# Transposing key and query weights by DMA from DRAM, issuing early loads from two queues, and a new order of work in a conditioned transformer block

## The chip, the cores and the metric

The kernel runs on one core of one Trainium2 chip. The metric is device time in microseconds (us) of one launch. Three runs of the kernel before took 207.98, 208.01 and 208.36 us, so the median is 208.01.

A core has five engines that run their own instruction queues side by side: PE (matrix products; its weight loads are listed apart as PEld), DVE (vector work), ACT (scalar functions and copies), POOL (further elementwise work) and SP, which here only issues DMA transfers. ACT can issue transfers too. Each engine works through its queue strictly in order and waits at an instruction until the semaphores that it names have arrived.

## What is computed

A block with 2048 tokens of width 512: a first half with linear attention over 32 heads of 16 columns, a second half with a gated layer of width 1376. A condition vector c gives six modulation vectors.

```python
mod = (silu(c) @ w_mod).reshape(1, 6, 1, -1)          # sa, ca, ga, sb, cb, gb
h = layernorm(x) * (1 + ca) + sa
q, k, v = heads of h @ wqkv
pq, pk = q @ w_phi, k @ w_phi                         # 16x16 per head
phi = concat(softmax(p), softmax(-p))                 # for q and for k
kv, z = phi_k.T @ v, phi_k.sum(tokens)
x = x + ga * ((phi_q @ kv) / (phi_q @ z) @ wo)
h = layernorm(x) * (1 + cb) + sb
x = x + gb * ((sigmoid(h @ w_gate) * (h @ w_up)) @ w_down)
```

## The kernel before

**Tiling.** Tokens are cut into 16 tiles of 128. x, all weights and the normalised, transposed h1T stay in on-chip memory. Keys and queries use weights that are folded first: wqk_f is wk (or wq) times the block-diagonal matrix bd of w_phi, so that one product gives pk directly.

**The order is written out by hand.** Every piece of work is a task in a graph: `G.add(name, {engine: cost}, fn, r=..., w=..., bufs=...)` names the engines that may run it, what it reads and writes and which buffers it holds. The long string `ORDER` (lines 37 to 78) lists every task once; `arrange` walks it, gives each task the engine after its `@` (or the first of its table) and hands out buffer slots first come, first served, and `emit` then writes the instructions. So each engine's queue is the ORDER string filtered by engine. The costs in the tables play no part when the kernel runs.

**DMA transfers.** `load` (line 659) makes a load task, always on SP. Each transfer signals one of eight semaphores, used in rotation; a transfer whose semaphore is still in use by an older one waits at its issuing engine until that older one has landed.

**The start.** ACT issues the loads of c and w_phi (lines 229 and 231) and loads its function table (line 232). PE runs dummy products (`warm`). The tasks that matter here:

- `ld_x0b`, `ld_x0a`, ... (lines 663, 664): x in pieces of two tiles. `st1_t` (lines 799, 800, DVE): mean and variance of tile t. `rs1_g` (806, 807 on ACT, 809, 810 on POOL) and `nmr1_g` (815, DVE): reciprocal deviation and shift of a group g of one or two tiles. `xn1_t` (824 ACT, 826 DVE, 828 POOL): the normalised tile. `tphgj` (841, PE) transposes column block j of group g, and `hm1_gj` (848 ACT, 850 DVE) applies the modulation on the way to h1T. Groups 6 and 7 are transposed by DMA instead (`xT1_t`, 833).
- `ld_wk0`, `ld_wk1` (670): the key weights. `tpwk` (759, PE) transposes them in blocks, `wTck` (763, ACT) copies the result to wT_sb. `fold1i` (776, PE) multiplies by bd, `foldc1i` (782 ACT, 784 DVE) writes wqk_f. Each fold reads all four wT blocks.
- `ld_wq0` (676), `wqTk` (769): the query weights, loaded and then transposed by DMA from on-chip memory to on-chip memory.
- `c1`, `c2`, `c3`: silu(c). `ld_wm00`, `ld_wm01` (667): the columns of w_mod for sa and ca, by halves of the rows. `modc1.0`, `modc1.1` (735, PE) and `modc1c` (741, 742, ACT): sa and 1 + ca.

**The attention stage.** Per tile: `Kt` (867, PE, four 512-column products, one for each row block j), `et` (883, ACT, two exponentials), `nt` (886, DVE, sums), `rt` (896, 897 on ACT or 899 on DVE, reciprocal), `phit` (889, POOL or DVE), `Vt` (871, PE), `vat` (907, ACT or DVE), `kvt` (280, PE, accumulates over all tiles). Queries: `Q` (945, PE), `qe` (950, ACT). When all 16 `kv` are in, `kvm` (301, DVE), `kvp` (316, PE) and the copies to kvbd follow.

**The rest.** For each tile numerators, division, projection with wo, second normalisation; then in six chunks of tokens g and u (574, PE), tanh (584, ACT), the product (595, DVE), y (612, PE), `fin` (619, DVE) and the store `st` (621, SP). `modc2.0`, `modc2.1` (735) compute the second set of modulation vectors. Tile 15's y is cut in 384 and 128 columns, and the 128 columns come last.

Of the kernel before, what the change touches and what calls it, by code (L numbers as in the profile page):

```python
# [38 lines left out]
wTc0 nmr1_2 st1_4 ld_wk1 tpw3 warm1_8 tpw2 wTc2 xn1_3@P bd ld_x2a st1_5 xn1_2@P nmr1_1 st1_0 warm1_9 warm1_10 warm1_11 warm1_12 wTc3 rs1_0 ld_wm00 ld_wm01  # L39
st1_9 c3 st1_8 xn1_0 warm1_13 warm1_14 fold11 ld_x2b fold13 fold12 fold10 modc1.0 ld_wv0 foldc11 foldc13 foldc10 modc1.1 tph20 rs1_3@P xn1_1@P ld_x1b rs1_5@P  # L40
foldc12@D modc1c tph21 tph11 tph22 warm1_15 nmr1_3 xn1_5@P xn1_4@P hm1_21 hm1_20@A hm1_22 tph03 tph23 tph10 tph01 tph00 hm1_10 hm1_23@A K2 hm1_00@A ld_wq0
tph02 hm1_01@A hm1_03@A ld_wd2 ld_wmga ld_x3a wqT2 nmr1_5 xn1_8@P xn1_9@P st1_10 st1_11 tph13 K3 tph12 rs1_6@P hm1_02@A hm1_11@A hm1_12 st1_7 tph33 tph30 K0
hm1_13@A wqT0 wqT3 wqT1 e2.0 st1_6 nmr1_6 hm1_33 n2.0 rs1_4@P e0.0 e3.0 hm1_30@A nmr1_4 tph32 V2 K1 tph53 V3 tph52 tph31 hm1_53 hm1_32 xn1_11@P hm1_31 e1.0
# [4 lines left out]
qe10 n7.0 r8.0 xn1_12@P xT1_12 va6@D r7.0 phi6.0 xn1_15@P tph83 kv5.0 ld_wg0 ld_wo tph80 kv6.0 tph81 hm1_83 e11.2 hm1_81 hm1_71@P phi7.0 hm1_72@A e10.0
hm1_70@A hm1_73@A V8 n9.0 hm1_80 V10 va8@D n10.0 e11.4 va9 r9.0@A phi8.0 e11.0 e11.6 n11.2 n11.0 r10.0 n11.6 V13 kv7.0 tph82 r11.6 r11.0 n11.4 hm1_82@A K12
K13 kv8.0 va10 e13.4 r11.2 ld_wu0 e13.0 phi9.0 n13.4 r11.4 r13.4 n13.0 e12.0 phi10.0 K15 Q11 ld_wd kv9.0 V14 phi11.0@D n12.0 e15.4 r13.0@A K14 kv10.0 phi11.2  # L50
phi11.4 phi11.6 e15.0 va13 Q03 Q01 e14.4 r12.0@A va14 e14.0 phi13.4@D phi13.0 phi12.0 n14.4 n14.0 r14.4@A r14.0 n15.0 n15.4 r15.4 phi14.4@D V12 kv11.4 Q13
modc2.0 va12 qe01 phi14.0 phi15.4@D qe13 r15.0@A kv11.0 kv11.6 kv11.2 gra kv12.0 V15 Q02 kv13.4 va15 qe03 phi15.0@D kv14.4 kv13.0 kv15.4 kv14.0 kvm1 kv15.0
Q32 kvm0 qe02 perm kvp2 kvp1 kvp0 kvz2 kvz1 kvz0 kvn0 modc2.1 sm0 sm2 qe32 modc2c kvn2@A kvn1@A wo2 smS2 smS0@D den0 den2 Q12 Q31 qe31 wo3 num00 qe11 num30
num01 Q30 num31 u00 u01 Q23 num20 u30 u31 qe12 u20 tpo0 num21 u21 oT0 wo1 wo0 wo_all sm1 smS1 o3 sm4 smS4 num10 out0 num11 den1 x1_0 qe30 qe23 Q33 Q21 Q22
num61 qe33 u11 st2_0 u10 o2 tpo1 rs2_0 gwb nmr2_0 den4 num70 u70 qe21 oT1 num71 xn2_0 u71 grb wd0 qe22 Q20 out1 wd10 xnT0 num60 x1_1 mod00 mod01 wd4 wd5 wd1
# [24 lines left out]
bndc u5.10 u5.3 hm5.9 hm5.8 y11.9 y11.10 bndd u5.1 tg5.3 tg5.1 hm5.3 fin11 hm5.1 g5.10 ldf y12.0 y14.0 y14.1 y14.2 y14.3 y14.4 y14.5 y14.6 y14.7 y14.8 y14.9  # L80
# [77 lines left out]
def kernel(  # L158
# [92 lines left out]
    def engine(e):  # L251
        return {"PE": pe, "ACT": act, "DVE": dve, "POOL": pool, "SP": sp}[e]
# [406 lines left out]
    def load(name, key, fn, nbytes):  # L659
        G.add("ld_" + name, {"SP": 0.45}, fn, w=key, nbytes=nbytes)  # L660
# [473 lines left out]
```

## Time and profile before

| | |
|---|---|
| median of 3 runs | 208.01 us |
| the profiled execution | 208.63 us |
| its span, first to last instruction | 206.9 us |
| busy of PE, DVE, ACT, POOL | 199.4, 168.8, 110.1, 96.3 us |
| granted PE clock | 0.999 |
| moved by DMA | 19.27 MB |

The span begins with the first instruction and ends with the last; 1.73 us of the device time lie around it. The sums of the prediction are made in the span of the profiled execution. In the views an entry gives the start (us from the span's start), the busy time (us), the engine, the source line and what is written and read; "SPq" and "ACTq" are the issues of transfers on those queues, and "idle before" names what the engine waited for last.

### The profile page before, as it was taken

How to read it: one execution, taken by the hardware profiler on the slowest of the kernel's cores; microseconds unless marked ns; L12 is line 12 of the kernel's file. 1: busy time of each engine (PE TensorE's matmuls, PEld its weight loads, DVE VectorE, ACT ScalarE, POOL GpSimd, SP SyncE). 2: the span in 40 equal slices, each digit the busy share in tenths (PEclk: the TensorE clock that was granted, in tenths of full speed). 3: DMA queues.
4: the chain of work that ended last, by engine and by line, in shares of the span. 5: the costliest groups of instructions: out<-in, count | busy, mean ns of one | idle time of the engine just before them, and what ended most of it. 6: DMA issues, size and time to landing. Idle time of an engine off the chain costs nothing.

```text
span 206.9 us, 4373 instructions
## 1 busy us (share of the span) xinstructions
PE 199.4 (96%) x1539; PEld 112.8 (54%) x1563; DVE 168.8 (82%) x462; ACT 110.1 (53%) x267; POOL 96.3 (47%) x128
## 2 busy tenths in 40 slices
PE   7889999999999999999999999999999999999993
PEld 2465554554676689768764544454444444444442
DVE  3999999998989998999999999898797865235632
ACT  2689999999979986433343543231523351144100
POOL 5787999999976987774256000014400220000000
PEclk9999999999999999999999999999999999999999
DMA  6999877697101211205321121141223022000111
GB/s 161 341 351 237 106 194 261 183 382 242 55 0 54 51 32 25 54 0 103 72 49 34 39 42 25 26 91 39 52 51 76 5 51 76 0 0 29 33 52 54
DMA packets 32557, 19.27 MB, mean 93 GB/s; under 512 B 21169, under 2 KB 30738, under 8 KB 32530
## 3 DMA queue, kind: packets, MB, share of 16 engines
q1 hardware_dynamic: 32000, 18.92, 34.3%
q8 instruction: 14, 0.23, 0.5%
q14 instruction: 13, 0.11, 0.2%
q10 hardware_dynamic: 530, 0.02, 0.1%
HBM read 12.11 MB, written 2.10 MB: 69 GB/s over the span
## 4 chain that ended last, share of the span: by engine, by line
PE 71%; ACT 18%; DMA 4%; DVE 3%; SPq 2%; issue 1%; DVEq 0%; ACTq 0%
PE y_ps L612 18%; PE u_ps L574 17%; PE g_ps L574 17%; ACT e L883 8%; PE a_ps L483 7%; PE q_ps L945 4%; ACT h1T L848 4%; DMA wmod_sb<-in_w_mod_dram 4%; ACT vaug L907 3%; PE num L366 2%; PE num L450 2%; DVE phi L889 1%; PE g_ps L576 1%; SPq L664 1%; DVE ks L886 1%
## 5 line engine op out<-in xcount | busy, mean ns | idle before, releaser
L584 ACT ACTIVATE tg<-g_ps 128x512 bf16<-128x512 f32 (+5 forms) x66 | 28.9, 454 | 58.0 <-PE g_ps L574 38.1
L612 PE MATMUL y_ps<-wd_sb,wmod_sb 128*128 128x512 bf16 (+4 forms) x184 | 43.8, 366 | 0.2
L595 DVE SCALAR_TENSOR_TENSOR wmod_sb<-tg,u_ps 128x512 bf16<-128x512 bf16 (+4 forms) x63 | 30.0, 494 | 15.0 <-ACT tg L584 7.3
L574 PEld LDWEIGHTS <-wu_sb 128*128 128x128 bf16 (+1 forms) x252 | 21.7, 99 | 15.7 <-issue 0.2
L574 PEld LDWEIGHTS <-wg_sb 128*128 128x128 bf16 (+1 forms) x252 | 21.5, 99 | 14.7 <-issue 0.2
L889 POOL TENSOR_TENSOR phi<-e,ks 128x1024 bf16<-128x1024 bf16 (+2 forms) x17 | 27.7, 1637 | 1.1 <-DVE ks L899 0.3
L612 PEld LDWEIGHTS <-wmod_sb 128*128 128x128 bf16 (+1 forms) x187 | 17.4, 98 | 16.9 <-issue 0.2
L574 PE MATMUL u_ps<-wT_sb,wu_sb 128*128 128x512 bf16 (+2 forms) x122 | 23.7, 321 | 0.1
L574 PE MATMUL g_ps<-wT_sb,wg_sb 128*128 128x512 bf16 (+2 forms) x122 | 23.7, 321 | 0.1
L503 POOL TENSOR_SCALAR ve<-mv 128x2 f32<-128x2 f32 (+1 forms) x8 | 1.8, 223 | 42.3 <-DVE mv L493 42.3
L574 PE MATMUL u_ps<-wqk_sb,wu_sb 128*128 128x128 bf16 (+4 forms) x127 | 19.9, 287 | 0.1
L886 DVE TENSOR_REDUCE ks<-e 128x64 f32<-128x1024 bf16 (+2 forms) x22 | 19.7, 903 | 0.3 <-ACT e L883 0.2
L574 PE MATMUL g_ps<-wqk_sb,wg_sb 128*128 128x128 bf16 (+4 forms) x127 | 19.6, 287 | 0.1
L883 ACT ACTIVATE e<-k_ps 128x512 bf16<-128x512 f32 (+2 forms) x44 | 18.4, 500 | 0.0
L950 ACT ACTIVATE eT<-q_ps 128x512 bf16<-128x512 f32 x32 | 16.8, 611 | 1.8 <-PE q_ps L945 1.7
L474 POOL TENSOR_TENSOR o<-u 128x512 bf16<-128x512 f32 x10 | 12.6, 1269 | 9.5 <-DVE u L456 4.2
L619 DVE TENSOR_TENSOR ot<-y_ps,x 128x512 bf16<-128x512 f32 (+2 forms) x17 | 11.2, 656 | 6.9 <-PE y_ps L612 6.6
L483 PE MATMUL a_ps<-wo_sb,oT 128*128 128x512 bf16 x57 | 15.7, 379 | 0.4
L945 PE MATMUL q_ps<-h1T,wqk_f 128*128 128x512 bf16 x62 | 15.7, 379 | 0.1
L867 PE MATMUL k_ps<-wqk_f,h1T 128*128 128x512 bf16 x63 | 15.5, 379 | 0.1
L871 PE MATMUL v_ps<-wv_sb,h1T 128*128 128x512 bf16 x59 | 15.2, 379 | 0.2
L799 DVE BATCH_NORM_STATS2 st<-x_sb 128x6 f32<-128x512 bf16 x16 | 10.8, 673 | 2.6 <-DMA x_sb<-in_A_x_dram 2.6
(156 smaller groups left out, 334.7 us busy)
## 6 DMA issues: line engine op xcount, KB each, us to landing
out_dram<-ot SPq DMA_DIRECT2D x15, 128.0 KB, 1.8
x_sb<-in_A_x_dram SPq DMA_DIRECT2D x6, 256.0 KB, 5.0
wmod_sb<-in_w_mod_dram SPq DMA_DIRECT2D x3, 512.0 KB, 6.5
wmod_sb<-in_w_mod_dram SPq DMA_DIRECT2D x1, 1536.0 KB, 10.3
wg_sb<-in_B_w_gate_dram SPq DMA_DIRECT2D x1, 1376.0 KB, 7.1
wd_sb<-in_B_w_down_dram SPq DMA_DIRECT2D x1, 1280.0 KB, 13.9
wu_sb<-in_B_w_up_dram SPq DMA_DIRECT2D x1, 768.0 KB, 11.0
wu_sb<-in_B_w_up_dram SPq DMA_DIRECT2D x1, 608.0 KB
```

Source lines behind the costliest of these rows:

```text
L483: pe.matmul(ap_[:], lhsT=oT[:, j, :], rhs=wo_sb[:, j, :], start=(j == 0), stop=(j == KT - 1))
L574: pe.matmul(ps[:fsz, 0:n], lhsT=w[:, j, ft * P:ft * P + fsz], rhs=h[:, j, 0:n], start=(j == 0), stop=(j == KT - 1))
L584: G.add(f"tg{k}.{ft}", {"ACT": 0.13 + n * 0.00083}, lambda e, tg=tg, g_ps=g_ps, fsz=fsz, n=n: act.activation(tg[:fsz, 0:n], g_ps[:fsz, 0:n ...
L595: dve.scalar_tensor_tensor(hm_all[:fsz, hm[k].slot, ft, 0:n], tg[:fsz, 0:n], 1.0, u_ps[:fsz, 0:n], op0=ALU.add, op1=ALU.mult)
L612: mm = pe.matmul(y[:, 0:c1 - c0], lhsT=hm_all[:fsz, hm[k].slot, ft, tl * P:(tl + 1) * P], rhs=wd_sb[:fsz, ft, c0:c1], start=(ft == 0), sto ...
L867: pe.matmul(kp[:], lhsT=h1T[:, j, t * P:(t + 1) * P], rhs=wqk_f[:, j, D:2 * D], start=(j == 0), stop=(j == KT - 1))
L871: pe.matmul(vp[:], lhsT=h1T[:, j, t * P:(t + 1) * P], rhs=wv_sb[:, j, :], start=(j == 0), stop=(j == KT - 1))
L883: act.activation(ee[:, ha:hb, s, :], kp[:, ha * DH:hb * DH].rearrange("p (h j) -> p h j", j=DH), ACT.Exp, scale=1.0 - 2.0 * s)
L886: dve.tensor_reduce(ks[:, ha:hb].rearrange("p h s -> p (h s)"), ee[:, ha:hb].rearrange("p h s j -> p (h s) j"), axis=AX.X, op=ALU.add)
L889: engine(e).tensor_tensor(ph[:, ha * 32:hb * 32].rearrange("p (h j) -> p h j", j=DH), ee[:, ha:hb].rearrange("p h s j -> p (h s) j"), ks[: ...
L945: pe.matmul(qp[:], lhsT=wqk_f[:, j, blk * P:(blk + 1) * P], rhs=h1T[:, j, cq * 512:(cq + 1) * 512], start=(j == 0), stop=(j == KT - 1))
L950: act.activation(eT[cq][:, s * 4 + blk, :], qp[:], ACT.Exp, scale=1.0 - 2.0 * s)
```

## The change

- **Weights straight from DRAM** (`DIRECT = [1, 1]`). `ld_wk0`, `ld_wk1`, `tpw0` to `tpw3`, `wTc0` to `wTc3` and `ld_wq0` go. Instead `wkT0` to `wkT3` and `wqT0` to `wqT3` are DMA transposes on SP that read 128 rows of A_wqkv in DRAM and write one row block of wT_sb for all head columns. A fold now waits for its own row block only.
- **Two issuing queues.** The loads of x and of the first modulation weights may stand on ACT. In the new order ACT issues `ld_x0a`, `ld_x1a`, `ld_wm00a`, `ld_wm00b`, behind c and w_phi; the function table load becomes a task `actl` and stands behind them.
- **Modulation by column halves.** `ld_wm0ih` loads 256 columns of sa (a) or ca (b); `modc1.h` and `modc1ch` finish two of the four column blocks each, and `hm1_gj` waits for its half only. An array `mone` lets DVE do `modc1ch`; the order leaves it on ACT.
- **Products in halves.** `K0` to `K7` and `V0` to `V3` become `Kta`, `Ktb` (row blocks 0 and 1, then 2 and 3), each waiting for its own blocks.
- **Smaller loads**: wv, w_gate, x3 and wo in two pieces each, w_down's ten full blocks in two.
- **A new ORDER** for every engine. Among its moves: `phi9.0` and `phi12.0` (full tiles) and `phi11.4`, `phi14.0`, `phi15.0`, `phi15.4` stand on DVE (before: `phi11.0`, `phi13.4`, `phi14.4`, `phi15.0`, `phi15.4`); `xn1_13` and `xn1_15` stand on DVE; both halves of `modc2` stand ahead of `kv15`; the y products of tile 14 now come last.

```diff
+KSP = 8
+DIRECT = [1, 1]
+VSP = 4
-SPLIT = {"wk": 2, "wv": 1, "wq": 1, "wg": 1, "wu": 2, "x1": 2, "x2": 2, "x3": 1}
+SPLIT = {"wk": 2, "wv": 2, "wq": 2, "wg": 2, "wu": 2, "x1": 2, "x2": 2, "x3": 2, "wo": 2}
...
-wdz warm0 pmem ld_x0b st1_2 st1_3 ld_x0a c1 warm1_0 warm1_1 warm1_2 warm1_3 warm1_4 warm1_5 warm1_6 warm1_7 st1_1 c2 rs1_2 rs1_1 ld_x1a ld_wk0 tpw1 tpw0 wTc1
+wdz warm0 c1 warm1_0 warm1_1 warm1_2 warm1_3 warm1_4 warm1_5 warm1_6 warm1_7 warm1_8 warm1_9 warm1_10 warm1_11 ld_x0a@A pmem bd ld_x0b st1_2 st1_3 ld_x1a@A
+ld_wm00a@A ld_wm00b@A wkT1 wkT2 st1_1 st1_0 wkT0 actl ld_wm01a rs1_2 rs1_1 c2 nmr1_1 nmr1_2 xn1_2@P fold12 fold11 warm1_12 c3 rs1_0 xn1_3 xn1_1@P tph21
+modc1.0 ld_x2a foldc12 foldc11 modc1c0 st1_4 st1_5 tph10 tph20 tph13 tph11 warm1_13 ld_wm01b xn1_0 hm1_20 rs1_3@P tph00 tph02 warm1_14 tph03 fold10 hm1_00
+hm1_11@A hm1_21@A hm1_10@A wkT3 ld_x1b warm1_15 tph22 tph23 tph01 ld_x2b modc1.1 nmr1_3 xn1_5@P xn1_4@P foldc10 K3a hm1_01@A modc1c1 hm1_03@A hm1_22@A st1_8
...
-    act.preload_act_table_set("natural_log_exp_and_others")
...
+        G.add("ld_" + name, {"SP": 0.45, "ACT": 0.45} if act else {"SP": 0.45}, fn, w=key, nbytes=nbytes)
...
+        for s in range(2):
+            c = s * D + 256 * i
+            load(f"wm0{i}{'ab'[s]}", [("wmod0", i, s)], lambda e, c=c: engine(e).dma_start(wmod_sb[:, :, c:c + 256], wmod_v[:, :, c:c + 256]), 256 * K1, True)
...
+    G.add("actl", {"ACT": 1.19}, lambda e: act.preload_act_table_set("natural_log_exp_and_others"), w=["actl"])
...
+            if side == 1 and DIRECT[1]:
+                G.add(f"wkT{k}", {"SP": 1.2}, lambda e, k=k: sp.dma_start_transpose(wT_sb[:, 1, :, k * P:(k + 1) * P], A_wqkv[k * P:(k + 1) * P, D:2 * D]),
+                      w=[("wT", 1, k)], nbytes=-1)
...
+                if DIRECT[0]:
+                    G.add(f"wqT{k}", {"SP": 1.2}, lambda e, k=k: sp.dma_start_transpose(wT_sb[:, 0, :, k * P:(k + 1) * P], A_wqkv[k * P:(k + 1) * P, 0:D]),
+                          w=[("wT", 0, k)], nbytes=-1)
...
-            G.add(f"fold{side}{kt_in}", {"PE": 0.24}, f3, r=[("wT", side, k) for k in range(KT)] + ["bd"], w=[("fold", side, kt_in)], bufs=[ps])
+            G.add(f"fold{side}{kt_in}", {"PE": 0.24}, f3, r=[("wT", side, kt_in), "bd"], w=[("fold", side, kt_in)], bufs=[ps])
...
+        if t < KSP:
+            for h in range(2):
+                js = (2 * h, 2 * h + 1)
+                G.add(f"K{t}{'ab'[h]}", {"PE": 0.435}, lambda e, js=js, f=f_k: f(e, js), r=[h1k[j] for j in js] + [("wqk", j, 1) for j in js], w=[("k", t)], bufs=[kp])
```

The instructions on PE that do the computation stay the same but for the 16 transposes of `tpw`.

More of the change, by code (lines that the diff above doesn't have):

```diff
@@ L40 @@
[L40 to L43, printed above, removed]
@@ L48 @@
[L48 to L51, printed above, removed]
@@ L52 @@
[L52 to L55, printed above, removed]
@@ L738, in modc_task, with modc1_task, f, f2 @@
         G.add(nm + "c", {"ACT": dur}, lambda e: f2(ps), r=[nm + "ps"], w=wk, bufs=[ps])
-    def f_mc1(ps):
-        act.copy(modc[:, 0:4], ps[:, 0:4])
-        act.add(modc[:, 4:8], ps[:, 4:8], 1.0)
+    def modc1_task(h):
+        ps = bank("modc_ps", [P, 2, 2])
+        dst = modc[:, 0:8].rearrange("p (s j) -> p s j", s=2)[:, :, 2 * h:2 * h + 2]
+        def f(e):
+            for j in range(KT):
+                for s in range(2):
+                    for i in range(2):
+                        c = s * D + (2 * h + i) * P
+                        pe.matmul(ps[:, s, i:i + 1], lhsT=wmod_sb[:, j, c:c + P], rhs=sc_bf[:, j:j + 1],
+                                  start=(j == 0 and s == 0 and i == 0), stop=(j == KT - 1), skip_group_check=True)
+        def f2(e):
+            if e == "ACT":
+                act.copy(dst[:, 0], ps[:, 0])
+                act.add(dst[:, 1], ps[:, 1], 1.0)
+            else:
+                dve.tensor_tensor(dst, ps[:], mone[:], op=ALU.add)
+        G.add(f"modc1.{h}", {"PE": 0.4}, f, r=[("wmod0", h, 0), ("wmod0", h, 1), "scbf"], w=[("mc1ps", h)], bufs=[ps])
+        G.add(f"modc1c{h}", {"ACT": 0.35, "DVE": 0.15}, f2, r=[("mc1ps", h)], w=[("mod1", h)], bufs=[ps])
     def f_mc2(ps):
@@ L810, in f_rs @@
                 pool.tensor_tensor(rs1[:, sl], ve1[:, sl], mhalf[:, sl], op=ALU.pow)
-        G.add(f"rs1_{g}", {"ACT": 0.43, "POOL": 1.1}, f_rs, r=[("mv1", t) for t in ts], w=[("rs1", g)])
+        G.add(f"rs1_{g}", {"ACT": 0.43, "POOL": 1.1}, f_rs, r=[("mv1", t) for t in ts] + ["actl"], w=[("rs1", g)])
         if g:
```

147 lines of the change are left out of this document (82 added, 65 removed).

## Prediction

> **What bounds the kernel now.** I read the page first: busy times, then the chain of work that ended last.
>
> ```profile
> PE 199.4 (96%) x1539; PEld 112.8 (54%) x1563; DVE 168.8 (82%) x462; ACT 110.1 (53%) x267; POOL 96.3 (47%) x128
> PE 71%; ACT 18%; DMA 4%; DVE 3%; SPq 2%; issue 1%; DVEq 0%; ACTq 0%
> ```
>
> PE carries 71% of the chain, but it is an average over stages. The chain in order of time shows them:
>
> ```profile
> 4.45 7.29 DMA wmod_sb<-in_w_mod_dram
> 11.79 0.57 PE modc_ps L735 x16
> 12.65 3.19 ACT h1T L848 x8
> ...
> 53.10 1.32 DVE phi L889
> 54.54 1.34 DVE phi L889 x2
> 56.23 0.86 PE q_ps L945 x4
> 57.10 0.50 PE kvp L316 x16
> 57.60 0.66 PE modc_ps L735 x24
> ...
> 194.16 9.56 PE y_ps L612 x55
> ```
>
> The start waits for modulation weights (to 11.79). The attention stage then runs on ACT and ends on three DVE phi; from 56.23 to the last y at 203.7 there is nothing but PE. The windows say how tight each stage is (columns: length, then busy time of PE, PEld, DVE, ACT, POOL):
>
> ```profile
> 13.84:55.80 41.96, 41.28 (x364) 22.98 (x368) 40.22 (x84) 41.40 (x108) 39.51 (x38) 1.00 0.80 217
> 3.62:55.80 52.18, 50.12 (x462) 28.41 (x468) 49.57 (x114) 48.10 (x126) 46.23 (x49) 1.00 0.85 240
> 56.00:203.70 147.70, 146.80 (x1072) 83.53 (x1089) 118.50 (x347) 60.50 (x141) 47.22 (x60) 1.00 0.18 42
> ```
>
> From 13.84 to 55.80 all four engines are busy over 94% of the time. That is the key to this change: in this stage an earlier start of PE returns nothing unless DVE, ACT and POOL also end earlier. After 56 PE idles visibly for 147.70 - 146.80 = 0.90 us, so a better order there can return about that.
>
> **The front.** Timeline of the first stage (start, busy), then what the tile and line views say of landings:
>
> ```profile
> 0.80 1.48 SPq L664 DMA_DIRECT2D x_sb<-in_A_x_dram  x3
> 1.36 0.44 ACTq L231 DMA_DIRECT2D wp_sb<-in_A_w_phi_dram  x1
> 1.84 1.28 ACT L232 ACT_TABLE_LOAD   x1 [1.84 <-issue]
> 3.62 0.69 DVE L799 BATCH_NORM_STATS2 st<-x_sb 128x6 f32<-128x512 bf16 x1 [2.43 <-DMA x_sb<-in_A_x_dram]
> 4.45 0.66 DVE L799 BATCH_NORM_STATS2 st<-x_sb 128x6 f32<-128x512 bf16 x1
> 5.42 0.30 ACT L806 ACTIVATE ve<-mv,eps 128x2 f32<-128x2 f32 x1 [1.05 <-DVE mv L800]
> 6.15 0.29 ACT L806 ACTIVATE ve<-mv,eps 128x1 f32<-128x1 f32 x1 [0.20 <-DVE mv L800]
> 10.28 1.56 ACT L782 CAST wqk_f<-fold_ps 128x512 bf16<-128x512 f32 x3
> 13.49 0.81 PE L867 MATMUL k_ps<-wqk_f,h1T 128*128 128x512 bf16 x3
> ```
>
> ```profile
> L769 SPq DMA_TRANSPOSE wT_sb<-wqk_sb x4: 1266/1274/1335, 16.4 to 20.3; - x4
> DMA to landing us min/median/max: 2.9/4.2/5.3
> ```
>
> ```profile
> L833 SPq DMA_TRANSPOSE h1T<-xn x4: 1189/1230/1268, 21.7 to 35.7; - x4
> DMA to landing us min/median/max: 2.4/2.4/3.2
> ```
>
> Now the new queue of ACT: c, w_phi (issued until 1.80), x0a, x1a, wm00a, wm00b, the table load, and only then rs1_2. In the built program wm00a waits until x0b has landed and wm00b until wkT1 has, because the eight transfer semaphores are used in turn. x0b is still SP's first issue and lands at 3.62, where the first statistics start. wkT1 is SP's second: issued from 0.80 + 1.48/3 = 1.29 on, for 1.27 us. Its landing is the unknown of this stage, since no trace shows a transpose that reads DRAM: the rows of transposes that read on-chip memory give 2.4 to 5.3 us. I take 3.2, the slowest of the h1T rows, since wkT1 has a load of x in front of it as well, and keep 2.4 and 5.3 as ends. So wkT1 lands at 4.5, wm00b is issued until 5.0, the table is loaded at 6.3 (in before it was hidden, 1.84 to 3.12), and rs1_2 starts at 6.3 instead of 5.42: **0.9 later**.
>
> What follows on ACT ahead of K3a: three pairs of rs1 (5.42 to 6.15 less the 0.20 waited is 0.53 each, 1.6), c2 (0.2), xn1_3 (0.8, row below), foldc12, foldc11, foldc10 (1.56/3 each, 1.6), a modc pair (about 0.3) and three hm1 of one or two tiles (3.19/8 each, 1.2): 5.7 in all, so K3a starts near 12.0, against 13.49. PE's front is 1.5 earlier. What goes (16 tpw transposes, 4 wTc copies, two key loads) lay beside the wait for w_mod. SP's four wkT cost 4 x 1.27 = 5.1 us of issue ahead of the later x loads, wv and the rest; x2a is issued near 5.6 instead of 3.38, and its readers st1_8 and st1_9 come after 11. That is cover enough as long as x2a lands within 5.4 us; beyond that DVE would wait by the difference. Halves of K and V move no work, the 128 products stay; they let K start on two row blocks.
>
> **The stage on DVE.** DVE starts at 3.62 as before, and I count what the new order gives it. Groups by form (count | busy us, mean ns):
>
> ```profile
> L850 DVE TENSOR_SCALAR h1T<-tp_h,modc 128x256 bf16<-128x256 bf16 x11 | 4.1, 394 | 0.6 <-ACT modc L742 0.3 <-PE tp_h L841 0.2
> L899 DVE RECIPROCAL ks<-ks 128x64 f32<-128x64 f32 x7 | 3.8, 542 | 0.1
> L889 DVE TENSOR_TENSOR phi<-e,ks 128x512 bf16<-128x512 bf16 x4 | 3.3, 855 | 0.7 <-POOL phi L889 0.5
> L824 ACT ACTIVATE xn<-x_sb,nmr,rs 128x512 bf16<-128x512 bf16 x2 | 1.6, 812 | 0.0
> L850 DVE TENSOR_SCALAR h1T<-h1T,modc 128x256 bf16<-128x256 bf16 x3 | 1.0, 383 | 0.0
> L826 DVE TENSOR_SCALAR xn<-x_sb,mv,rs 128x512 bf16<-128x512 bf16 x1 | 0.4, 381 | 0.0
> ```
>
> ```profile
> L889 DVE TENSOR_TENSOR phi<-e,ks x5: 424/693/1311, 47.0 to 55.2; 128x512 bf16<-128x512 bf16 x4, 128x256 bf16<-128x256 bf16 x1
> ```
>
> It loses one half phi (0.86), one reciprocal (0.54), one h1T out of PSUM (0.39) and two h1T in place (0.77): -2.56. It gains two xn (0.76) and two full-tile phi (phi9, phi12). A full phi on DVE isn't in the trace; it is twice a half one: 2 x 0.69 to 2 x 1.31, at the mean 1.71. So DVE's work grows by 0.76 + 3.42 - 2.56 = **+1.6** (bounds +1.0 and +3.4). The half phi took 0.69 where DVE had waited for POOL's to end, and 1.31 at 53.10, with POOL's own phi running.
> The Trainium skill, "SBUF — State Buffer", section "Who interferes with whom", has the reason: a DVE instruction with two on-chip inputs and a POOL instruction that reads on-chip memory exclude each other, and the later one blocks. The two lengths agree with it. By that page a full phi could wait out a whole POOL phi on top and the sum would end above my upper bound.
>
> DVE's idle time was 52.18 - 49.57 = 2.61, of which 41.96 - 40.22 = 1.74 after 13.84. At the front the four first statistics end at 3.62 + 4 x 0.8 = 6.8, and nmr1_1 now waits for rs1_1 at 6.3 + 2 x 0.53 = 7.4: +0.6. Of the 1.74 I let 1.1 go, since DVE is now behind everyone and its waits for POOL's phi (0.5 in its row) shrink as POOL gives two phi away. That is a choice; the bounds are 0 and all 1.74. So the last phi ends 1.6 + 0.6 - 1.1 = **1.1 later**, near 56.9. ACT doesn't relieve this: its modulation starts about 2.5 earlier, but it takes one fold copy, two v copies, three more reciprocal pairs and another rs1 pair, some 3 to 4 us, and ends later too. POOL's relief (two phi) helps nobody, as it doesn't end last.
>
> So PE's 1.5 earlier start turns into waiting at the last kv products.
>
> **After the stage.** One half of modc2 (0.66, the chain's row at 57.60) has moved ahead of kv15, into that waiting: **-0.66**. Tail, from the view of the output tile and of the transfers:
>
> ```profile
> L619 DVE TENSOR_TENSOR ot<-y_ps,x x6: 291/688/692, 192.7 to 203.7; 128x512 bf16<-128x512 f32 x4, 128x384 bf16<-128x384 f32 x1, 128x128 bf16<-128x128 f32 x1
> ```
>
> ```profile
> out_dram<-ot SPq DMA_DIRECT2D x15, 128.0 KB, 1.8
> ...
> out_dram<-ot SPq DMA_DIRECT2D x1, 32.0 KB, 1.8
> ```
>
> Before, the last y is 128 columns wide and its fin takes 0.29; now it is a whole tile, 0.69: **+0.40**. The stores land in 1.8 either way. The other loads (w_gate, wo, w_down in pieces, wq without its copy) are hidden: after 56 the DMA engines are busy 18%.
>
> **Sum:** +1.1 - 0.66 + 0.40 = +0.8 on the profiled 208.63 (1.73 outside its span of 206.9). The median of the runs shown is 0.62 lower: 208.01 + 0.8 = **208.8**.
>
> **Rivals.**
> 1. *Faster: DVE keeps up.* If its full phi cost only 1.38 and all later idle time goes, the stage ends 1.0 + 0.6 - 1.74 = 0.1 earlier; if the new order also returns half of PE's visible 0.90, the sum is -0.1 - 0.66 + 0.40 - 0.45 = -0.8: 207.2. For it: POOL has slack now, so the exclusion can resolve in DVE's favour. It decides where the last phi ends less than 0.26 later than before. PE's whole 1.5 can't come through: DVE would have to do 49.57 + 1.6 in 50.7 us.
> 2. *Much slower: transposes from DRAM land late.* At the 5.3 us of the wT_sb row wkT1 lands 2.1 later; ACT stands in front of wm00b, the table and rs1_2 wait behind it, and all of DVE behind rs1_1: +2.1, so 210.9. For it: x0a, x1a and wm00a load at the same time.
> The Trainium skill, "VectorE: DVE Perf Modes", section "The three transpose paths", gives 1309 ns for a 128x128 transpose by DMA and 390 ns on TensorE; by an estimate from that page a wkT, four such blocks, would take 5.2 us. In this trace 2.4 for four blocks speaks against it.
> 3. *The change doesn't do what it says:* ACT's waits for landings cost as much as its issues save, DVE's extra work hides, and the rest cancels: 208.0.
>
> **Chances.** Forecast 0.42 (own range 207.6 to 209.7), rival 1 0.33, rival 2 0.18, rival 3 0.07. A measurement of this kernel tells 0.2%, 0.42 us, from no change. Faster by more: 0.31 of rival 1 and 0.02 of the forecast, 0.33. Within: 0.12 of the forecast, 0.02 of rival 1, 0.06 of rival 3, 0.20. Slower: 0.47. The range leaves out the ends of rivals 1 and 2: 206.4 to 210.9.
>
> **What would show it.** Right: rs1_2 on ACT near 6.3 behind the table load; first K near 12; the last phi on DVE after 56.3, PE waiting at kv13 to kv15 for DVE; modc2 before that; a last fin of 0.69. Wrong: the last phi at 55.5 or earlier (rival 1); rs1_2 after 7.5, wkT landing over 4.5 us (rival 2). The sum is also wrong if PE's idle time after the stage changes by over 1 us.

## The result: 4.9% slower, and the profile after

The changed kernel takes 218.25 us (217.88 to 218.68), the kernel before in the same session 208.10 (207.98 to 208.36): a ratio of 1.0485, interval 1.0465 to 1.0504. The forecast was 208.8 with a range up to 210.9. The direction, slower, was forecast; about 9.4 us are missing.

The page of the kernel after (busy times, the chain by engine, the granted clock in 40 slices):

```profile
PE 202.3 (94%) x1522; PEld 113.0 (52%) x1547; DVE 168.9 (78%) x453; ACT 107.8 (50%) x272; POOL 99.0 (46%) x133
PEclk9967999999999999999999999999999999999999
PE 68%; DVE 16%; DMA 9%; POOL 3%; issue 2%; SPq 0%; ACT 0%; POOLq 0%; DVEq 0%; ACTq 0%
```

ACT has left the chain (18% before, 0% now); DVE and DMA have taken its place (16% and 9%, before 3% and 4%), and the clock dips in two slices of the start. The chain in order of time says which transfers those are:

```profile
1.32 5.66 DMA wT_sb<-in_A_wqkv_dram
7.00 5.96 DMA wmod_sb<-in_w_mod_dram
...
17.13 7.97 DMA wmod_sb<-in_w_mod_dram
25.15 0.29 PE modc_ps L745 x4
...
62.82 1.66 DVE phi L926
```

Three landings stand in a row: the first key transpose, then a load of w_mod that was issued only when that had landed, then the 1536 KB load of w_mod (wmm2), for which matmuls of modca (the task that computes the modulation vector ga) waited until 25.15. The windows (columns as in the prediction, then granted clock, share of the DMA engines and GB/s) up to and after the last phi, first of the kernel after, then of the kernel before:

```profile
0.00:64.40 64.40, 55.35 (x475) 30.11 (x482) 52.65 (x114) 50.23 (x136) 47.84 (x71) 0.95 0.73 185
64.60:212.80 148.20, 146.86 (x1047) 82.84 (x1065) 115.41 (x339) 57.36 (x137) 50.99 (x63) 1.00 0.20 45
```

```profile
0.00:55.80 55.80, 52.50 (x467) 29.15 (x474) 49.84 (x115) 49.38 (x127) 48.89 (x68) 1.00 0.82 233
```

The last phi ends 8.6 later (64.5 against 55.9); the span is 9.2 longer (216.1 against 206.9), so 0.6 arises after it. Of the 8.6, DVE works 52.65 - 49.84 = 2.8 longer and stands idle 11.75 - 5.96 = 5.8 longer. Two more windows of the kernel after say where:

```profile
3.50:26.30 22.80, 17.24 (x141) 9.79 (x142) 15.01 (x45) 14.25 (x37) 11.68 (x22) 0.85 1.15 290
26.30:64.40 38.10, 35.86 (x332) 19.59 (x335) 37.36 (x68) 35.99 (x101) 33.61 (x31) 1.00 0.49 129
```

DVE idles 22.80 - 15.01 = 7.79 from 3.50 to 26.30 and only 0.74 after that, so the idle part is the start. Timeline of the kernel after, ACT's entries first, then SP, DVE and PE:

```profile
3.52 3.86 ACTq L674 DMA_DIRECT2D wmod_sb<-in_w_mod_dram  x2
7.41 1.28 ACT L699 ACT_TABLE_LOAD   x1 [7.41 <-DMA wT_sb<-in_A_wqkv_dram]
8.70 0.30 ACT L838 ACTIVATE ve<-mv,eps 128x2 f32<-128x2 f32 x1
...
17.13 0.47 SPq L688 DMA_DIRECT2D wmod_sb<-in_w_mod_dram  x1
...
6.81 0.69 DVE L831 BATCH_NORM_STATS2 st<-x_sb 128x6 f32<-128x512 bf16 x1 [1.59 <-DMA x_sb<-in_A_x_dram]
...
13.01 0.53 PE L759 MATMUL modc_ps<-sc_bf,wmod_sb 128*128 128x1 bf16 x14 [1.66 <-DMA wmod_sb<-in_w_mod_dram]
17.03 0.59 PE L899 MATMUL k_ps<-wqk_f,h1T 128*128 128x512 bf16 x1
25.15 0.29 PE L745 MATMUL modc_ps<-sc_bf,wmod_sb 128*128 128x1 bf16 x4 [0.92 <-DMA wmod_sb<-in_w_mod_dram]
```

ACT is held at the second of its two w_mod loads (wm00b) until wkT1 has landed, loads the table at 7.41 and begins rs1_2 at 8.70, 3.3 later than before (5.42). x0a, issued by ACT, reaches DVE at 6.81. wm00b lands at 13.0, and the first K starts at 17.03 instead of 13.49.

### The profile page after: what moved, and what is told of

Read it like the earlier page. It is cut to its first block, busy times and chain, and to the rows that moved or that the text cites. A ratio compares the mean times of both kernels' runs of the same rounds, so it can differ in the third digit from the quotient of the medians.

```text
span 216.1 us, 4342 instructions
## 1 busy us (share of the span) xinstructions
PE 202.3 (94%) x1522; PEld 113.0 (52%) x1547; DVE 168.9 (78%) x453; ACT 107.8 (50%) x272; POOL 99.0 (46%) x133
## 4 chain that ended last, share of the span: by engine, by line
PE 68%; DVE 16%; DMA 9%; POOL 3%; issue 2%; SPq 0%; ACT 0%; POOLq 0%; DVEq 0%; ACTq 0%
PE y_ps L617 17%; PE u_ps L579 16%; PE g_ps L579 16%; DMA wmod_sb<-in_w_mod_dram 6%; DVE ks L923 6%; PE a_ps L488 6%; PE q_ps L987 4%; DMA wT_sb<-in_A_wqkv_dram 3%; DVE phi L926 2%; PE num L371 2%; POOL phi L926 2%; PE num L455 2%; DVE ks L936 1%; PE g_ps L581 1%; DVE st L831 1%
## 5 line engine op out<-in xcount | busy, mean ns | idle before, releaser
L589 ACT ACTIVATE tg<-g_ps 128x512 bf16<-128x512 f32 (+4 forms) x66 | 29.0, 453 | 52.8 <-PE g_ps L579 35.9
L617 PE MATMUL y_ps<-wd_sb,wmod_sb 128*128 128x512 bf16 (+4 forms) x180 | 42.0, 366 | 0.2
L926 POOL TENSOR_TENSOR phi<-e,ks 128x1024 bf16<-128x1024 bf16 (+2 forms) x16 | 24.4, 1532 | 4.4 <-DVE ks L936 1.6
L479 POOL TENSOR_TENSOR o<-u 128x512 bf16<-128x512 f32 x13 | 16.4, 1269 | 15.9 <-DVE u L444 6.5
L579 PE MATMUL g_ps<-wT_sb,wg_sb 128*128 128x512 bf16 (+2 forms) x123 | 23.0, 322 | 0.1
L579 PE MATMUL g_ps<-wqk_sb,wg_sb 128*128 128x256 bf16 (+4 forms) x128 | 19.6, 287 | 0.1
L579 PE MATMUL u_ps<-wqk_sb,wu_sb 128*128 128x128 bf16 (+4 forms) x126 | 18.8, 286 | 0.1
L899 PE MATMUL k_ps<-wqk_f,h1T 128*128 128x512 bf16 x62 | 17.4, 391 | 0.6 <-DVE h1T L882 0.3
L903 PE MATMUL v_ps<-wv_sb,h1T 128*128 128x512 bf16 x61 | 16.2, 379 | 0.1
L976 POOL TENSOR_TENSOR wd_sb<-wd_sb,wmod_sb 128x512 bf16<-128x512 bf16 x11 | 13.9, 1283 | 0.0
```

The source lines that it names most:

```text
L479: G.add(f"o{t}", {"POOL": 1.3, "DVE": 0.62}, lambda e, ub=ub, o=o: engine(e).tensor_tensor(o[:], ub[0][:].rearrange("p h d -> p (h d)"), u ...
L579: pe.matmul(ps[:fsz, 0:n], lhsT=w[:, j, ft * P:ft * P + fsz], rhs=h[:, j, 0:n], start=(j == 0), stop=(j == KT - 1))
L589: G.add(f"tg{k}.{ft}", {"ACT": 0.13 + n * 0.00083}, lambda e, tg=tg, g_ps=g_ps, fsz=fsz, n=n: act.activation(tg[:fsz, 0:n], g_ps[:fsz, 0:n ...
L617: mm = pe.matmul(y[:, 0:c1 - c0], lhsT=hm_all[:fsz, hm[k].slot, ft, tl * P:(tl + 1) * P], rhs=wd_sb[:fsz, ft, c0:c1], start=(ft == 0), sto ...
L899: pe.matmul(kp[:], lhsT=h1T[:, j, t * P:(t + 1) * P], rhs=wqk_f[:, j, D:2 * D], start=(j == 0), stop=(j == KT - 1))
L926: engine(e).tensor_tensor(ph[:, ha * 32:hb * 32].rearrange("p (h j) -> p h j", j=DH), ee[:, ha:hb].rearrange("p h s j -> p (h s) j"), ks[: ...
```

## The experiments

The first theory (A) was that the DRAM transposes land late and hold ACT. Its rivals were the loads issued beside them (B) and the new order in the middle of the stage (C). Times are medians, and a ratio is taken to the kernel before, which was run again beside each set (the letter of a label names its set). Its medians there go from 207.76 to 208.14, so a comparison across sets is uncertain by some 0.4 us. The start also differs between profiled runs of the same order there: rs1_2 begins at 8.70 in the kernel after and at 7.90 in f1_mm2_late, which issues the same up to then.

**e1_wkT_chip**

```diff
- sp.dma_start_transpose(wT_sb[:, 1, :, k * P:(k + 1) * P], A_wqkv[k * P:(k + 1) * P, D:2 * D])
+ sp.dma_start_transpose(wT_sb[:, 1, :, k * P:(k + 1) * P], wd_sb[:, FT - 1, :])
...
```

> The changed kernel, but the four key transposes read a zeroed tile on the chip instead of DRAM (so the keys are computed from zero weights; every instruction and its size stays). Theory A, late transposes: reading DRAM is what makes them land 4.1 to 8.0 us after issue; from on-chip memory they land in 2.4 to 3.2, wkT1 near 4.5, the table load near 5.0, rs1_2 near 6.3 instead of 8.70, first K near 13 instead of 17.03, and about 4 us return: 214. Theory B, the loads issued beside them (x0a, x1a, wm00a, wm00b) slow any transfer of this stage: landings stay above 4.5 us and the time within 1 us of 218.2. Theory C, the middle of the order: the front gets earlier as in A, but DVE gives it back as idle time before the last phi: 216.5 to 218.

218.73, ratio 1.0491 (1.0440 to 1.0542). The view of the line that issues the key transposes, first in the kernel after, then here:

```profile
L783 SPq DMA_TRANSPOSE wT_sb<-in_A_wqkv_dram x4: 1189/1266/1280, 1.3 to 9.3; - x4
DMA to landing us min/median/max: 4.1/5.6/6.6
```

```profile
L783 SPq DMA_TRANSPOSE wT_sb<-wd_sb x4: 1191/1263/1286, 1.3 to 7.9; - x4
DMA to landing us min/median/max: 5.1/5.4/5.6
```

A transpose that reads on-chip memory lands just as late at this place (median 5.4 against 5.6). Theory A's reason falls: it is not the reading of DRAM that makes them late here.

**e2_keys_pe**

```diff
-ld_wm00a@A ld_wm00b@A wkT1 wkT2 st1_1 st1_0 wkT0 actl ld_wm01a rs1_2 rs1_1 c2 nmr1_1 nmr1_2 xn1_2@P fold12 fold11
+ld_wm00a@A ld_wm00b@A ld_wk0 ld_wk1 st1_1 st1_0 actl ld_wm01a rs1_2 rs1_1 c2 nmr1_1 nmr1_2 xn1_2@P tpw1 tpw2 wTc1 wTc2 tpw0 wTc0 tpw3 fold12 fold11 wTc3
...
-DIRECT = [1, 1]
+DIRECT = [1, 0]
```

> One part undone: the key weights are loaded in two pieces (in the place of the first two transposes) and transposed on PE again, 16 transposes and four copies on ACT; queries and all the rest as in the changed kernel. Theory A: nothing holds ACT to 7 us and the fold waits for no late transpose, first K near 13.5, 4 us return, less about 1 for four more copies of 0.53 on ACT: 215. Theory B: ACT's issues still wait for older transfers and x0a still lands near 6.8, so less than 1.5 us return: 217 or more. Theory C: 216.5 to 218, with DVE's last phi still over 6 us later than in the kernel before.

219.18, ratio 1.0552 (1.0514 to 1.0589): nothing returns, though the table load stands 2.3 earlier than in the kernel after and the first K 1.4 earlier. PE waits 1.63 at modca here.

**e3_all_sp**

```diff
-... ld_x0a@A pmem bd ld_x0b st1_2 st1_3 ld_x1a@A ld_wm00a@A ld_wm00b@A wkT1 ...
+... ld_x0a pmem bd ld_x0b st1_2 st1_3 ld_x1a ld_wm00a ld_wm00b wkT1 ...
```

> The other part undone: all loads of x and of w_mod stand on SP again, in the same order, so ACT issues only c and w_phi and loads its table at once; the transposes still read DRAM. Theory A: rs1_2 is back near 5.4, but the key transposes are issued some 2 us later (behind x0a, x1a and two w_mod pieces) and land as late as before, so the fold waits until 11 and little returns: 216.5 to 218.5. Theory B: about 4 us return: 214. Theory C: 216.5 to 218.

218.34, ratio 1.0501 (1.0472 to 1.0531). The timeline of this run shows why, ACT's entry first, then PE's:

```profile
6.15 0.29 ACT L838 ACTIVATE ve<-mv,eps 128x2 f32<-128x2 f32 x1 [3.04 <-DVE mv L832]
...
12.78 1.02 PE L899 MATMUL k_ps<-wqk_f,h1T 128*128 128x512 bf16 x4
24.91 0.29 PE L745 MATMUL modc_ps<-sc_bf,wmod_sb 128*128 128x1 bf16 x4 [4.97 <-DMA wmod_sb<-in_w_mod_dram]
```

For PE the start is mended: the first K stands at 12.78, 0.7 ahead of the kernel before. PE then waits 4.97 at modca, again to about 25. What the start gains is lost at that one wait, so all three theories missed the cause; that 218.34 lies in theory A's range is luck.

**e4_q_chip**

```diff
-DIRECT = [1, 1]
+DIRECT = [0, 1]
...
-... ld_x3a ld_wmm2 wqT1 ...
+... ld_x3a ld_wmm2 ld_wq0 wqT1 ...
```

> The query weights are loaded and then transposed from on-chip memory again, as in the kernel before; all the rest as in the changed kernel. Queries are first needed near 42 us. Theories A and B: their transposes have time, within 0.5 us of 218.2. Theory C: the four query transposes of the changed kernel take the transfer queues from wm and wv between 17 and 25 us, where PE waits for w_mod until 25.15: up to 1 us returns, 217.2.

217.96, ratio 1.0484 (1.0440 to 1.0527): the query part of the change is neutral, within the interval.

These four led to **theory D**: the new order puts `ld_wmm2` ahead of `modca`. In the built program the weight load of modca's second row block names the semaphore that wmm2's landing raises, though modca reads the columns of ga, which another load brings. The load of ga itself can't be what was missing: it is one transfer for all row blocks, and the first row block's matmuls had run (four at 23.97). (Why the program takes the two for overlapping wasn't tried. In the addresses, the first block's columns lie ahead of the first element that wmm2 writes and the second block's between the rows that it writes, so a comparison of whole spans would give just this wait.) wmm2 is 1536 KB, issued at 17.13, and lands 8.0 later. The kernel after and e1 to e4 fit: in all five the second row block starts between 24.43 and 25.28, whether the first K starts at 12.78 or at 17.03.

**f1_mm2_late**

```diff
-... ld_x3a ld_wmm2 wqT1 e1.0 V1b ... modca.0 V3b modca.1 rs1_6@P
+... ld_x3a wqT1 e1.0 V1b ... modca.0 V3b modca.1 ld_wmm2 rs1_6@P
```

> The changed kernel with one task moved: the load of the last 1536 KB of w_mod (wmm2) stands behind modca in the order instead of ahead of it. Theory D (formed on the traces of the first experiments): modca's matmuls of the second row block wait for that whole load although they read other columns, and where the front is early this wait alone sets when the stage goes on (5.0 us of PE in the run with all loads on SP). Here the front is late as well (first K at 17.0), so only the 0.92 us that PE waited in the changed kernel return: 217.2. Theory C, the middle of the order is slow by itself: no change, 218.2.

215.34, ratio 1.0371 (1.0336 to 1.0406): 2.9 return by the medians and 2.4 by the ratios, more than the 0.92 expected. Some 0.8 of it is the earlier start of this run (first K at 16.28), which the edit can't reach. The rest is more than PE's own wait: from 3.5 to 26.3 DVE gets 16.72 us of work done here against 15.01, ACT 15.71 against 14.25, so they had waited behind it too.

**f2_sp_mm2** (the edits of e3_all_sp and f1_mm2_late together)

> Both together: all loads of x and w_mod on SP, and wmm2 behind modca; the transposes still read DRAM. Theory D: the late front and the wait for wmm2 lie in series and cover each other, so each cure alone gave nothing and both together give about 5.5 us: 218.3 less the 5.0 of PE's wait and some of DVE's 6.0: 212.8, the rest above the kernel before being DVE's extra work of 2.8. Theory C: another wait takes the place, 216 or more.

212.05, ratio 1.0207 (1.0178 to 1.0237). On PE and DVE:

```profile
13.58 1.02 PE L899 MATMUL k_ps<-wqk_f,h1T 128*128 128x512 bf16 x3
19.59 0.40 PE L745 MATMUL modc_ps<-sc_bf,wmod_sb 128*128 128x1 bf16 x8
...
54.65 3.85 DVE L926 TENSOR_TENSOR phi<-e,ks 128x512 bf16<-128x512 bf16 x3
```

modca runs at 19.59 without a wait. The first cure alone gave nothing, the second 2.4 to 2.9, both together 6.2 (5.8 by the ratios): two late things that cover each other.

**f3_sp_mm2_pe** (as f2_sp_mm2, with the edit of e2_keys_pe)

> As the run with all loads on SP and wmm2 late, but the keys loaded and transposed on PE again. It tells what the DRAM transposes of the keys are worth once nothing hides it. Theory A, late transposes cost: 1 to 2 us faster than with them. Theory D: within 1 us of it, either way.

214.55, ratio 1.0335 (1.0310 to 1.0360). Neither expectation: with nothing else in the way, the transposes from DRAM, with the work that they take off PE and ACT, are worth 2.5 us. The first K starts at 15.12 here, against 13.58.

**f4_before_mm2**

```diff
-ld_x3a wqT2 nmr1_5 ... foldc01 va1 ld_wu1 ld_wmm2 tph41
+ld_x3a ld_wmm2 wqT2 nmr1_5 ... foldc01 va1 ld_wu1 tph41
```

> The kernel before with one task moved: wmm2 right behind ld_x3a, ahead of modca, as the changed kernel has it. Theory D: modca, at 20 us in the kernel before, now waits until wmm2 has landed near 25, and 3 to 4.5 us are lost: 211 to 212.5. Theory C: within 0.5 us of 208.0.

214.81, ratio 1.0343 (1.0300 to 1.0387): moving this one load costs the kernel before about 7 us, nothing else being changed, and more than the 3 to 4.5 expected. Its timeline on PE:

```profile
18.32 0.29 PE L734 MATMUL modc_ps<-sc_bf,wmod_sb 128*128 128x1 bf16 x4
23.69 0.46 PE L734 MATMUL modc_ps<-sc_bf,wmod_sb 128*128 128x1 bf16 x9 [5.07 <-DMA wmod_sb<-in_w_mod_dram]
```

Four matmuls (the first row block) run, then PE waits 5.07. This shows theory D in the other direction. Why a wait of 5.07 costs 7 was not separated: the granted clock also falls to 0.50 around 22 to 26, and the second pair of h1T transposes on SP comes 6 us later (40.02 against 34.03).

**g1_wd_behind** (f2_sp_mm2, and)

```diff
-... grb wd0 wd7 kv13.0 ... den0 wd2 num00 ... den2 wo_all wd10 ...
+... grb kv13.0 ... den0 num00 ... den2 wo_all wd0 wd7 wd2 wd10 ...
```

> The run with all loads on SP and wmm2 late, and POOL's three scalings of w_down (wd0, wd7, wd2) moved behind the scalings of wo, so that POOL reads no on-chip memory while DVE runs its last phi. Theory D with the exclusion of DVE and POOL as the price of the last phi: the three half phi of 3.85 us from 54.65 shrink to 3 x 0.69 = 2.1 or a little more, 1.2 to 1.7 us return: 210.6. Rival: DVE's length comes from the two inputs alone, no change: 212.0.

210.28, ratio 1.0117 (1.0075 to 1.0159). In f2_sp_mm2 POOL scaled w_down during the last phi (its timeline, first fence); here DVE runs the same three phi with POOL quiet (timeline of g1_wd_behind, second fence):

```profile
54.78 4.75 POOL L976 TENSOR_TENSOR wd_sb<-wd_sb,wmod_sb 128x512 bf16<-128x512 bf16 x3
```

```profile
54.94 1.92 DVE L926 TENSOR_TENSOR phi<-e,ks 128x512 bf16<-128x512 bf16 x3
```

3.85 become 1.92, a little less than expected, and 1.8 us of the time return. The kernel after has the same pair (DVE's three phi from 60.61 take 3.85, POOL's three scalings from 60.73 take 4.75). DVE's whole work up to the last phi (third number) is now close to the 49.84 of the kernel before:

```profile
0.00:56.80 56.80, 52.40 (x478) 28.50 (x479) 50.00 (x114) 48.24 (x132) 44.43 (x68) 1.00 0.80 209
```

**g2_phi_pool**, **g3_phi3_pool** (g1_wd_behind, and)

```diff
-phi12.0@D ... phi14.0@D
+phi12.0@P ... phi14.0@P
```

(g3: `phi9.0@P` as well.)

> As g1_wd_behind, with phi12.0 (a full tile) and phi14.0 (a half) on POOL instead of DVE. Theory D: what was left over the kernel before is DVE's work (52.08 us up to the last phi against 49.84), and POOL has room once w_down is out of its way: DVE loses 1.13 and 0.7 to 1.3, so 1.8 less again, 208.8. Rival: POOL's phi (1.93 and 1.06) now end last, 210.6 or more.

> As g2_phi_pool, with phi9.0 on POOL as well. DVE loses another 1.21, POOL gains 1.93. Theory D, the two engines level: 207.7 to 208.8. Rival: POOL is now the one that ends last and nothing more returns, 209 or more.

213.23, ratio 1.0262 (1.0226 to 1.0299), and 213.87, ratio 1.0270 (1.0232 to 1.0308): 3 us worse than g1_wd_behind, the rival. (Their expectation counted 52.08 us of DVE work as still there, but 50.00 were left.) In the waits of g2_phi_pool PE now waits for POOL's phi:

```profile
PE kvacc L285 <- POOL phi L926: 2.1, 2, 1.3
```

In two places, 2.1 us in all: POOL has idle time on average, but not ahead of the last kv products.

**g4_before_wkT**

```diff
-ld_x1a ld_wk0 tpw1 tpw0 wTc1 wTc0 ... ld_wk1 tpw3 ... tpw2 wTc2 ... ld_x2a ... wTc3 ... ld_wm00 ld_wm01
+ld_x1a ld_wm00 wkT1 wkT3 ld_wm01 ld_x2a wkT2 wkT0 ...
```

> The kernel before with one part of the change alone: the keys transposed by DMA from DRAM (in the issue order x0b, x0a, x1a, wm00, wkT1, wkT3, wm01, x2a, wkT2, wkT0), no key loads, no transposes on PE, no four copies on ACT, each fold waiting for its own block; all else, the order included, as before. Theory D: the part itself is no loss, but SP's 5.1 us of issues put wm01 and the last wkT about 1 us later and DVE and ACT fill the stage as before: within 1 us of 208.0. Theory A, late transposes cost: 2 us or more slower, 210.

212.63, ratio 1.0212 (1.0187 to 1.0238): the part alone costs 4.6 here. That is theory A's price (2 us or more), not theory D's (within 1 us). On DVE and PE:

```profile
11.30 0.69 DVE L787 BATCH_NORM_STATS2 st<-x_sb 128x6 f32<-128x512 bf16 x1 [2.46 <-DMA x_sb<-in_A_x_dram]
...
11.89 0.41 PE L764 MATMUL fold_ps<-bd,wT_sb 128*128 128x128 bf16 x4 [2.79 <-DMA wT_sb<-in_A_wqkv_dram]
```

x2a comes 2.25 later (11.30 against 9.05), and DVE's c3, which modc1 needs, stands behind its statistics; the first K starts at 15.57 instead of 13.49. The same part is thus worth 2.5 in f3's comparison and costs 4.6 here, so its worth depends on the order around it. That its place in SP's queue decides is argued from these two waits; no run tests it, and the rest of the 4.6 is not traced.

**h1_act_x** (f1_mm2_late, and)

```diff
-ld_x1a@A ld_wm00a@A ld_wm00b@A wkT1 wkT2 st1_1 st1_0 wkT0 actl ld_wm01a
+ld_x1a@A actl ld_wm00a ld_wm00b wkT1 wkT2 st1_1 st1_0 wkT0 ld_wm01a
```

> As f1_mm2_late, with the hold taken from ACT: ld_wm00a and ld_wm00b stand on SP, the table load right behind ACT's two loads of x (x0a, x1a), which stay on ACT. Theory H, the hold makes the front late: rs1_2 at 5.4 to 6.5, first K near 13.5, and the 3.3 us between f1_mm2_late and f2_sp_mm2 return: 212. Rival, the loads of x from ACT's queue: x0a still lands near 6.8 and at most 1.3 returns, 214 to 215.

213.08, ratio 1.0231 (1.0181 to 1.0281): the hold is worth 2.3 of the 3.3 us between f1 and f2 by the medians, 2.9 of 3.4 by the ratios. rs1_2 is at 5.48. What remains, 1.0 or 0.5, lies within the intervals of h1 and f2, so it isn't shown. If it is there, x from ACT's queue is a candidate, since DVE waits for it longer than in f2_sp_mm2:

```profile
DVE st L831 <- DMA x_sb<-in_A_x_dram: 5.0, 2, 2.5
```

Two waits, 5.0 us in all; in f2_sp_mm2 they are 3.9.

**h2_x0b_first**, **h3_x0b_tail**

```diff
-... ld_x0a pmem bd ld_x0b st1_2 ...
+... pmem bd ld_x0b ld_x0a st1_2 ...
```

and for h3 also

```diff
-... fin15 st15 ldf y15.5b y15.6b ... fin15b st15b fin13 ... fin14 st14
+... fin15 st15 ldf ... fin13 ... fin14 st14 y15.5b y15.6b y15.7b y15.8b y15.9b y15.10b fin15b st15b
```

> As g1_wd_behind, with x0b issued first on SP (there x0a is first, and the first statistics, which need x0b, start 0.8 us later than in the kernel before). Expected: DVE starts 0.8 earlier, and with DVE full until the last phi 0.5 to 0.9 return: 209.5. Rival: another landing (x0a for st1_1) takes its place, no change, 210.3.

> As h2_x0b_first, with the 128-column piece of tile 15 (its last six y and its fin and store) moved to the end, as in the kernel before: the last fin takes 0.29 instead of 0.69, so 0.4 less than h2_x0b_first, 209.1. Rival: the piece's waiting bank costs as much, no change.

210.06, ratio 1.0106 (1.0070 to 1.0143), and 210.43, ratio 1.0128 (1.0086 to 1.0170). In h2 the last phi ends at 56.02, 0.84 earlier than in g1_wd_behind, but the medians differ by 0.2 only, which these intervals can't tell from nothing. In h3 the last two fins (a whole tile and the 128 columns, one entry below) don't follow their products; the first of them waits for the buffer that an older store still holds:

```profile
205.13 0.89 DVE L624 TENSOR_TENSOR ot<-y_ps,x 128x512 bf16<-128x512 f32 x2 [2.84 <-DMA out_dram<-ot]
```

DVE stood idle 2.84 for that store, so the 0.4 of the shorter fin did not come through.

**h4_probe**

```diff
+    for i in range(6):
+        G.add(f"pr{i}", {"SP": 1.2}, lambda e, i=i: sp.dma_start_transpose(wT_sb[:, 0, :, 0:P], h1T[:, 0, 0:512] if i % 2 else A_wqkv[0:P, D:2 * D]),
+              w=[("wT", 0, 0)], nbytes=-1)
-... gwa gra ...
+... gwa pr0 pr1 pr2 pr3 pr4 pr5 gra ...
```

> The changed kernel with six more transposes of 128x512 behind the store of the scaled gate vector (near 47 us, where hardly anything else is being moved), one after the other, each waiting for the one before to land; the first, third and fifth read A_wqkv in DRAM, the others h1T on the chip; their results are not used. If reading DRAM makes a transpose slow, the DRAM ones land 1 us or more later than the others' 2.4; if it is the other traffic of the start, both land in 2.4 to 3.0. The time is not of interest (the later loads on SP wait, 218 to 222).

219.06 in its one run. The issues on SP, each starting when the one before has landed:

```profile
47.05 1.35 SPq L824 DMA_TRANSPOSE wT_sb<-in_A_wqkv_dram  x1
52.92 1.19 SPq L824 DMA_TRANSPOSE wT_sb<-h1T  x1
55.32 1.19 SPq L824 DMA_TRANSPOSE wT_sb<-in_A_wqkv_dram  x1
58.03 1.19 SPq L824 DMA_TRANSPOSE wT_sb<-h1T  x1
60.47 1.19 SPq L824 DMA_TRANSPOSE wT_sb<-in_A_wqkv_dram  x1
64.18 1.19 SPq L824 DMA_TRANSPOSE wT_sb<-h1T  x1
```

Alone, the on-chip ones take 2.4 each (52.92 to 55.32, 58.03 to 60.47), the DRAM ones 2.7 and 3.7. The first one, issued while w_down and w_gate were still arriving, took 5.9. So by these few landings reading DRAM adds 0.3 to 1.3 us, and the other transfers add 2 to 3.

No version here beats the kernel before; the best, h2_x0b_first, is 1.1% slower. Its last phi ends at 56.02, where before it was 55.88, so the rest lies after the stage: its span is 1.0 longer (207.9 against 206.9), of which 0.7 lie between the last phi and the last y and 0.2 behind the last y. What makes the 0.7 stays open.

## Why the prediction was wrong, step by step

- **wmm2's move ahead of modca had no term; this is the first step that failed.** The sentence "The other loads (w_gate, wo, w_down in pieces, wq without its copy) are hidden" doesn't name wmm2, and the sum puts it at nothing without a reason. The prediction asked whether each load comes in time for its reader, not whether a load that nobody needs yet makes an earlier reader wait. No rival had it. Alone, moving it back returned 2.4 to 2.9; in the kernel before the same move cost 7; and it hides the rest, since the whole cure of the start was lost at modca (e3_all_sp).
- **The landing of wkT1, chosen at 3.2 after its issue, was 5.7** (the chain's first row), above even the upper end of 5.3; this is the second step. The sum of 5.7 us up to K3a also had no row for the landing of wm00b, 5.96 after its issue, for which modc1 waited until 13.01. So the first K stood at 17.03 instead of 12.0. Rival 2 had the mechanism word for word (ACT behind wm00b, the table and rs1_2 behind ACT) and its mark, rs1_2 after 7.5: it was 8.70. Its price of 2.1 is near the 2.3 to 2.9 that h1_act_x returned once modca no longer hid it. Of its reasons, the loads at the same time are borne out by e1_wkT_chip and h4_probe; reading DRAM, which it is named for, is not what made wkT1 late (e1_wkT_chip). The Trainium skill, "VectorE: DVE Perf Modes", section "The three transpose paths", led to an estimate of 5.2; the 5.7 looks like it, but the 2.4 to 3.7 of h4_probe show that four blocks alone do not take four times the page's 1309 ns.
- **x0a, now issued by ACT, was given no price.** It reached DVE at 6.81, where the prediction ended all four first statistics at 6.8. What that costs isn't shown: h1 against f2 leaves at most 1.0 for it, within the noise.
- **DVE's work, +1.6 with bounds +1.0 and +3.4, was +2.8.** That sign and bounds held is luck. A full phi took 1.21, not 1.71, and less than the 1.38 of the lower bound; with POOL's scalings out of the way (g1_wd_behind) DVE's work is 50.00, only 0.2 above the kernel before. Most of the growth lies in the last three half phi, which took 3.85 because POOL scaled w_down beside them; that these scalings now stand there was not counted. The Trainium skill, "SBUF — State Buffer", section "Who interferes with whom" (the exclusive lock), is borne out by g1_wd_behind: 1.92 without POOL against 3.85 beside it.
- **Idle time: +0.6 at the front, -1.1 later.** The later part came out about as chosen (0.74 after 26.30, where 0.64 of 1.74 were to be left after 13.84; the windows differ). The front's +0.6 is the term that was mis-sized: DVE's idle time grew by 5.8 in all. "POOL's relief (two phi) helps nobody" is contradicted by g2_phi_pool: with a full and a half phi back on POOL, PE waits 2.1 for it and 3 us are lost.
- **After the stage** the sum said -0.66 + 0.40. Measured is +0.6 up to the end of the span, of which 0.5 lie between the last phi and the last y. PE's visible idle time there is 148.20 - 146.86 = 1.34 against 0.90. modc2 did move ahead, but PE's busy time behind the stage is as long as before (146.86 against 146.80); why its 0.66 did not return stays open. The last fin did take 0.69 instead of 0.29, but from the last y to the end of the span it is 3.3 against 3.2, so only 0.1 of the +0.40 arrived. In h3, meant to take the 0.40 back, another wait took its place.
- **Some signs came true without the mechanism:** the last phi after 56.3 (64.5), PE waiting for it at the last kv, a last fin of 0.69. They fit any late stage, and say nothing of the 8.6. rs1_2 (8.70, not 6.3) and the first K (17.03, not 12) were the ones that told.

Of the 10.15 us, the loads back on SP and wmm2 behind modca together return 5.8 to 6.2 (f2_sp_mm2), the scalings moved out of DVE's way 1.8 (g1_wd_behind); some 2 are left in h2_x0b_first.

## What to carry to other kernels

When an order is rewritten, check every wait that each instruction carries in the built program, not only whether the data that it reads comes in time: a load moved ahead of a reader of the same tile can become its wait. Where two causes of lateness lie in series, undoing one may show nothing; try them together before dropping either. Don't let the engine that runs the critical work issue a transfer that may have to wait for an older one.

## What the runs showed of the hardware

- **Landing times go by the traffic.** A 128x512 transpose alone landed in 2.4 us from on-chip memory and in 2.7 and 3.7 from DRAM (h4_probe). At the start, beside the other loads, it took 5.1 to 5.6 from on-chip memory (e1_wkT_chip) and 4.1 to 6.6 from DRAM.
- **The granted clock fell when PE waited.** The windows of the kernel after (the column behind POOL is the granted clock):

```profile
8.00:10.80 2.80, 0.84 (x9) 0.51 (x9) 1.52 (x9) 2.65 (x9) 0.59 (x1) 1.00 1.19 287
10.80:13.50 2.70, 0.80 (x20) 0.72 (x21) 1.66 (x5) 1.15 (x3) 1.94 (x4) 0.74 1.19 297
13.50:16.20 2.70, 2.70 (x19) 1.75 (x17) 1.90 (x7) 1.85 (x6) 0.78 (x2) 0.50 1.10 349
16.20:18.90 2.70, 2.48 (x27) 1.60 (x26) 2.02 (x6) 1.78 (x6) 1.67 (x3) 0.50 1.10 342
18.90:21.60 2.70, 2.70 (x20) 1.50 (x19) 1.57 (x7) 2.36 (x6) 1.92 (x4) 0.99 1.05 385
```

PE was busy 0.84 and 0.80 in the first two and had the clock at 0.50 in the next two, just when the first K came. The Trainium skill, "TensorE: Matmul & The Clock Gate", section "Part 1: The HAM clock gate", says that an idle window of about 3.4 us halves the clock until one busy window has passed; these rows agree in kind, though PE was not wholly idle here (busy 1.64 of 5.5 us) and the clock stayed halved for nearly 7 us. e3_all_sp, with an early start but 4.97 of waiting at modca, falls to 0.50 as well (22 to 28). Its mean clock, that of f1_mm2_late (late start, no such wait) and that of the kernel after are all 0.983 to 0.984; f2_sp_mm2, with neither, has 0.997. So a long wait of PE is followed by slower products; how much of the time that costs, no run separates.
